# Linear attention and spectral mixing on one core: two tiles' sums placed ahead of the early rows, four filler products fewer, and the late rows gathered by two transfers

## The chip, the cores and the metric

The kernel runs on one core of one Trainium2 chip. A core has five engines with instruction streams of their own: TensorE (PE in the profile; its weight loads are PEld), VectorE (DVE), ScalarE (ACT), GpSimd (POOL) and SyncE (SP). Each engine takes its instructions in program order and waits on semaphores for the others. POOL and SP also issue DMA transfers, which 16 DMA engines of the core carry out. The metric is the device time of one execution in microseconds (us), the median over several; lower is better. TensorE's clock is granted by a throttle; the profile shows it as a share of full speed (PEclk).

## The reference

```python
def _attn_ref(q, k, v):                     # q, k, v: (8, 8, 576, 64)
    phi = lambda x: np.where(x > 0, x, np.exp(x) - 1.0) + 1.0
    q_p, k_p = phi(q), phi(k)
    kv = np.einsum('bhsd,bhse->bhde', k_p, v)
    num = np.einsum('bhsd,bhde->bhse', q_p, kv)
    den = np.einsum('bhsd,bhd->bhs', q_p, np.sum(k_p, axis=2))[..., None] + 1e-06
    return num / den

def _moe_ref(x, w_r, w_i, w_ch):            # x: (8, 576, 512), w_r, w_i: (64, 512, 512)
    X = np.fft.rfft(x, axis=1)
    Xr, Xi = np.real(X[:, :64]), np.imag(X[:, :64])
    Y = np.zeros_like(X)
    Y[:, :64] = (Xr @ w_r - Xi @ w_i) + 1j * (Xr @ w_i + Xi @ w_r)   # one 512x512 pair for each mode
    u = x + np.fft.irfft(Y, n=576, axis=1)
    return u + np.maximum(u @ w_ch, 0.0)    # (8, 576, 512), float32
```

The 64 modes' weights, w_r and w_i, are 64 x 2 x 1 MB of float32: 134 MB to be read once. The output is 9.4 MB.

## The kernel before

**Stages.** First the attention of the eight batches (lines 373 to 408), with the forward transform of its result into 64 modes. Then 32 pairs of modes: `mode_pair(p)` (L465) multiplies the spectrum by the weights of modes 2p and 2p+1. Weights come over POOL's DMA queue, which also turns them into bfloat16, into two rotating buffers. While weights are on their way, other work is done from a list, `work`, in slots after parts of each pair (`work_slot`, L427). That work rebuilds the attention output x, adds the inverse transform of the first 32 modes (`fold`), turns it (`turn_x`) and multiplies by w_ch (`channel_product`, kept as E). The last stage adds the modes 32 to 63 to x and to u @ w_ch, takes the rectifier and stores the output.

**Order.** Nearly all instructions are pinned to program order, so what stands earlier in the code is issued earlier on its engine. `keep_warm(n)` (L419) issues n products of 512 columns whose result nobody reads; in the profile they are the group at L422 (`zl<-wch,id`). `FILL[p]` says how many follow pair p, `WARM` how many follow each of the pieces in which the very last weights come.

**The last pair** (`last_pair`, L490) does modes 62 and 63. The weights of pair 31 come in eight transfers (`w_load_last`, L124): mode 62's two halves, mode 63's first half, and its second half in five pieces, `PIECES`, of two, two, two, one and one of the eight chunks. The steps on TensorE are: the early rows (`ahead_rows`, L920: the results of the modes 56 to 61, as rows in y and multiplied by w_ch in z, after VectorE has copied them into Y8 at L922); a slot of the list, whose first two items are the channel product and the first rows of the first pair of output tiles (`channels(0)` L807, `first_rows(0)` L900); the product of mode 62 (L435); a second slot with the same for the second pair of tiles; the picks (L458); three fillers; and then mode 63 piece by piece (L518, `y_last`), each piece after its weights have landed, with a filler after some.

**The late rows.** All late modes' rows must lie in one tile, YZ_all, ordered by batch, with y and z beside each other. Rows of modes 56 to 61 are gathered into it by two transfers (`ahead_gathers`, L940), one issued from SP and one from POOL, which wait for the third piece from the end. After mode 63 its rows are transposed (L978) and multiplied by w_ch (L984) into `last[0]` (y) and `last[1]` (z), and four transfers on POOL's queue (L994) bring the 32 rows of the modes 62 and 63 into YZ_all: z to both halves of the tile, then y to both. The output tiles of the first two batches do not read these rows from YZ_all but from `last` with their own selection matrix (`lead_sb`); the others read YZ_all (`add_inverse`, L762).

**The tail.** The tiles are finished in pairs: `channels` (L807), the late modes in z (L767), the rectifier on ACT (L1002, L817), the late modes in y (L767), the sum on VectorE (L1006, L841), and a store from SP's queue (L823, L829). The first four pairs are stored tile by tile in 256 KB, the others in 512 KB. There are 22 stores.

Of the kernel before, what the change touches and what calls it, by code (L numbers as in the profile page):

```python
# [11 lines left out]
F16 = mybir.dt.float16  # L12
# [31 lines left out]
def kernel(  # L44
# [10 lines left out]
    nc = tc.nc  # L55

    B, H, S, Dh = q.shape
    D = H * Dh
    NM = moe_w_r.shape[0]
    NHP = H // 2  # L60
    NDC = D // 128
# [8 lines left out]
    NA = NL - 2  # L70
    RA = 2 * B * NA
# [36 lines left out]
    pin = tc.keep_in_program_order  # L108
# [3 lines left out]
    LAST = NM // 2 - 1  # L112
# [41 lines left out]
    def rows_of(jj: int, base: int = 0):  # L154

        if jj < NJJ:
            return slice(base + jj, base + 512, NJJ)
        return slice(512, S) if base == 0 else slice(0, base)
# [252 lines left out]
    def w_get(p: int):  # L411
        if p not in w_in and p == LAST:
            w_load_last(wpool, "w", W_KEEP)
        elif p not in w_in:
            for half in range(2):
                w_load(p, half, wpool, "w", W_KEEP)
        return w_in[p]

    def keep_warm(n: int):  # L419

        for _ in range(n):
            pin(nc.tensor.matmul(last_ps[0], id16, wch16[:, 0, :]))  # L422
# [4 lines left out]
    def work_slot(p: int, name: str):  # L427
        for _ in range(slots.get((p, name), 0)):
            if work:
                work.pop(0)()  # L430

    def product(P, x, n: int, w, dc: int, n_dc: int):
        c = dc % NDC * 32
        pin(
            nc.tensor.matmul(  # L435
                P[c : c + n, :], x, w[:, dc, :],
                start=(dc < NDC), stop=(dc >= n_dc - NDC), tile_position=(0, c),
                skip_group_check=True,
            )
        )  # L440
# [24 lines left out]
    def mode_pair(p: int):  # L465
# [19 lines left out]
        work_slot(p, "end")  # L485
        keep_warm(FILL.get(p, 0))

    WARM = {2: 0, 4: 1, 6: 1, 7: 0, 8: 1}

    def last_pair():  # L490
        xl = ystage.tile([128, NDL, 2 * B], BF16, name="xl")
        for h in range(2):
            src = xt_v[:, (2 * h + 1) * NDC : (2 * h + 2) * NDC, :, :, LAST]
            pin(
                nc.vector.tensor_copy(
                    out=xl[:, h * NDC : h * NDC + NDC], in_=src.rearrange("p c t b -> p c (t b)")
                )
            )
        w = w_get(LAST)
        kk = NM - 2  # L500
        ahead_rows()
        work_slot(LAST, "start")
        P = psW.tile([128, D], F32, tag="P", bufs=2, name=f"P{kk}")
        for dc in range(NDL):
            n = 32 if dc < NDC else 2 * B
            product(P, xt_cols(dc, kk, n), n, w, dc, NDL)
        st = evacuate(kk, P)
        work_slot(LAST, "mid")
        picks(kk, st, 1)
        pin(nc.vector.tensor_copy(out=Y8[:, :, NA, :], in_=yt_ps[:, :, NA, :]))  # L510
        ahead_gathers()
        keep_warm(3)
        y_last = psW.tile([128, NDC, 2 * B], F32, tag="P", bufs=2, name="y_last")
        for piece in PIECES:
            for dc in range(piece.start, piece.stop):
                for ec in range(NDC):
                    pin(
                        nc.tensor.matmul(  # L518
                            y_last[:, ec, :], w[:, NDL + dc, ec * 128 : ec * 128 + 128], xl[:, dc, :],
                            start=(dc == 0 and ec == 0), stop=(dc == NDL - 1), skip_group_check=True,  # L520
                        )
                    )
            keep_warm(WARM[piece.stop])
        nc.vector.tensor_copy(out=Y8[:, :, NL - 1, :], in_=y_last)
# [12 lines left out]


    n_early = n_keep + n_pre
    FILL = {**{p: 7 for p in range(5, 16)}, **{p: 7 for p in range(18, 27)}, 27: 7, 28: 10, 29: 12, 30: 2}  # L540
    ystage = ctx.enter_context(tc.tile_pool(name="ystage", bufs=1, side="right"))
    inv_sb = ystage.tile([2 * NM, S], F16, name="inv_sb")
    inv2_sb = ystage.tile([128, S], F16, name="inv2_sb")
# [1 line left out]
    lead_sb = [ystage.tile([128, S], F16, name=f"lead{b}_sb") for b in range(N_LEAD)]  # L545
# [3 lines left out]
    Y8 = ystage.tile([128, NDC, NL, 2 * B], F16, name="Y8")  # L549
# [24 lines left out]
    yt_ps = None  # L574
# [9 lines left out]
    sW = ctx.enter_context(tc.tile_pool(name="sW", bufs=1))  # L584
# [11 lines left out]
    def x_of(t: int):  # L596
        if t < B * NJJ:
            return x_main[t // NJJ][:, t % NJJ, :]
        i = t - B * NJJ
        return x_tail[i // 2][:, i % 2, :]  # L600
# [13 lines left out]
    last_ps = []  # L614
# [65 lines left out]
        return ye_at[0]  # L680

    x16w, xTw = {}, {}

    def fold(t: int):

        x = x_of(t)
        acc = bank(f"ya{t}")
        for b, jj, orow in parts_of(t):
            pin(
                nc.tensor.matmul(  # L690
                    acc[orow, :], inv_sb[: 2 * NF, rows_of(jj, BASE[b % 2])], YE[b][: 2 * NF, :]
                )
            )
        pin(nc.vector.tensor_tensor(out=x, in0=acc, in1=x, op=ALU.add))  # L694
        x16w[t] = sW.tile([128, D], F16, tag="x16w", bufs=2, name=f"x16w{t}")
        pin(nc.scalar.copy(out=x16w[t], in_=x))  # L696

    def turn_x(t: int):
# [63 lines left out]
    def add_inverse(n: int, half: int, tiles_of=(0, 1)):  # L762

        def mm(i, orow, l, r):
            on_bank(
                n, {i},
                nc.tensor.matmul(  # L767
                    accs[n][orow, i], l, r, start=False, stop=True, skip_group_check=True
                ),
            )  # L770

        for i in tiles_of:
            for b, jj, orow in parts_of(pairs[n][i]):
                sel_rows = rows_of(jj, BASE[b % 2])
                if n < 2 * N_LEAD:
                    mm(i, orow, lead_sb[b][:, sel_rows], last[half])
                else:
                    g = HALVES[i]
                    mm(i, orow, inv2_sb[g, sel_rows], YZ[b][g, half, :])
# [139 lines left out]

    def ahead_rows():  # L920

        pin(nc.vector.tensor_copy(out=Y8[:, :, 0:NA, :], in_=yt_ps[:, :, 0:NA, :]))  # L922
        ya_ps = psW.tile([128, NDC, 128], F16, tag="P", bufs=2, name="ya_ps")
        za_ps = psW.tile([128, D], F32, tag="P", bufs=2, name="za_ps")
        for ec in range(NDC):
            pin(nc.tensor.transpose(ya_ps[:, ec, :], rows[ec], id16))
        for ec in range(NDC):
            pin(
                nc.tensor.matmul(
                    za_ps, rows[ec], wch16[:, ec, :], start=(ec == 0), stop=(ec == NDC - 1)  # L930
                )
            )
        pin(nc.scalar.copy(out=ahead[0:RA, 0, :], in_=ya_ps[0:RA].rearrange("p c r -> p (c r)")))
        pin(nc.scalar.copy(out=ahead[0:RA, 1, :], in_=za_ps[0:RA]))

    def late_at(h: int, r0: int, n: int):
        at = 64 * h + r0 // B * (NF // NL)
        return YZ_all[at : 64 * h + 64 : NF // NL][0 : n // B]
# [21 lines left out]
    for n in range(N_PRE):  # L960
# [1 line left out]
    last_pair()  # L962


    last = [
        sW.tile([128, D], F16, tag="x16w", bufs=2, name="last_y"),
        sW.tile([128, NDC, 128], F16, tag="xTw", bufs=2, name="last_z").rearrange("p c r -> p (c r)"),
    ]
    z1_ps = psW.tile([128, NDC, 8, 2 * B], F32, tag="yt", bufs=1, name="z1l")
    y_ps = [  # L970
        psW.tile([128, NDC, 128], F16, tag="P", bufs=2, name=f"ypl{h}")[:, 0 : NDC // 2] for h in range(2)
    ]
    y0 = psW.tile([128, D], F32, tag="P", bufs=2, name="y0l")
    last_ps.append(z1_ps.rearrange("p c m n -> p (c m n)"))
    hw = D // 2
    COLS = [slice(h * hw, h * hw + hw) for h in range(2)]
    for ec in range(NDC):
        pin(nc.tensor.transpose(y_ps[ec // 2][:, ec % 2, :], rows[ec], id16))  # L978
    pin(nc.scalar.copy(out=last[0][:, COLS[0]], in_=y_ps[0].rearrange("p c r -> p (c r)")))
    pin(nc.vector.tensor_copy(out=last[0][:, COLS[1]], in_=y_ps[1].rearrange("p c r -> p (c r)")))  # L980
    for h in range(2):
        for ec in range(NDC):
            pin(
                nc.tensor.matmul(  # L984
                    last_ps[h][:, 0:hw], rows[ec], wch16[:, ec, COLS[h]],
                    start=(ec == 0), stop=(ec == NDC - 1),
                )
            )
        pin(nc.scalar.copy(out=last[1][:, COLS[h]], in_=last_ps[h][:, 0:hw]))
    pin(nc.tensor.matmul(y0, lead_sb[0][:, rows_of(0)], last[0]))  # L990
    pin(nc.vector.tensor_tensor(out=x_of(0), in0=y0, in1=x_of(0), op=ALU.add))
    for z in (1, 0):
        for h in range(2):
            nc.gpsimd.dma_start(out=late_at(h, RA, 128 - RA)[:, :, z, :], in_=last[z][RA:128])  # L994
    psW.release()
    acc_pools.append(
        tc.alloc_tile_pool(name="psT1", bufs=1, space=PSUM, side="left", reuse_waits="tile")
# [11 lines left out]
    def sums_of(n: int, tiles_of):  # L1009
        channels(n, tiles_of)  # L1010
        add_inverse(n, 1, tiles_of)
        for i in tiles_of:
# [6 lines left out]
            out=x_of(0), in0=accs[0][:, 0], scalar=0.0, in1=x_of(0), op0=ALU.max, op1=ALU.add  # L1019
# [50 lines left out]
```

## Time and profile before

| what | value |
|---|---|
| median of three runs | 420.98 us (420.90 to 421.04) |
| profiled execution, its own time | 421.02 us |
| its span in the profile | 419.2 us |
| mean granted TensorE clock | 0.837 |
| PE busy | 313.1 us, 75% of the span, 3143 instructions |
| DVE busy | 231.2 us, 55% |
| ACT busy | 155.1 us, 37% |
| POOL's DMA queue | 81.54 MB, 93.6% of 16 engines' span |
| SP's DMA queue | 11.16 MB, 7.2% |
| read from and written to memory | 163.93 MB, 9.44 MB |

The profile is one execution. "Busy" sums an engine's instructions; matmuls are pipelined and their ends modelled, so a busy PE isn't a PE at its peak. The strip divides the span into 40 slices of 10.5 us and shows tenths. The chain of waits is followed back from the last instruction, at each step to what released it. The timeline lists instructions in order of time with start, length, engine, line, operation, tiles (out<-in) and how many were merged, and in brackets how long the engine stood idle before and what ended it.

### The profile page before, as it was taken

What the parts mean: (1) busy time and instruction counts of PE and PEld (TensorE: products, weight loads), DVE (VectorE), ACT (ScalarE), POOL (GpSimd) and SP (SyncE); (2) the same over time, 40 slices, a digit from 0 to 9 for tenths busy, and PEclk for the clock granted to TensorE, in tenths of its full rate; (3) what the DMA queues carried; (4) which work ended last, traced back from release to release, by engine and by line L of the source; (5) the groups of instructions that cost most, each with busy time, mean ns of one, the idle gap of its engine ahead of it and who ended that gap; (6) DMA issues with size and microseconds to landing.
All of it is one profiled execution on the core that took longest, in us unless ns stands there. A gap on an engine that the chain in (4) does not pass through costs nothing.

```text
span 419.2 us, 7479 instructions
## 1 busy us (share of the span) xinstructions
PE 313.1 (75%) x3143; PEld 162.6 (39%) x3143; DVE 231.2 (55%) x511; ACT 155.1 (37%) x255; POOL 59.1 (14%) x104
## 2 busy tenths in 40 slices
PE   0369997999607774777666686988788877998993
PEld 0257775877301331223222233333333323363421
DVE  4588899695414572464645353464446443532794
ACT  4687797854201020000000233344353423231783
POOL 4222224210011211111111111111111111130200
PEclk9999998579855687555856599899999989799998
DMA  8999999999999999999999999999999999999698
GB/s 217 212 212 217 209 224 203 228 208 222 213 227 205 223 219 208 224 217 209 220 216 214 220 209 220 217 212 220 220 208 220 217 213 220 213 202 177 229 394 331
DMA packets 17229, 93.17 MB, mean 222 GB/s; under 512 B 2284, under 2 KB 3196, under 8 KB 13036
## 3 DMA queue, kind: packets, MB, share of 16 engines
q0 software_dynamic: 12688, 81.54, 93.6%
q1 hardware_dynamic: 4508, 11.16, 7.2%
q8 instruction: 24, 0.39, 0.3%
q14 instruction: 9, 0.07, 0.0%
HBM read 163.93 MB, written 9.44 MB: 414 GB/s over the span
## 4 chain that ended last, share of the span: by engine, by line
DMA 60%; PE 24%; DVE 6%; issue 3%; ACT 3%; POOL 3%; DVEq 0%; ACTq 0%; POOLq 0%
DMA w<-in_moe_w_i_dram 48%; DMA pick_sb<-row_pick 8%; PE P L435 7%; DMA k<-in_k_dram 3%; PE acc L767 3%; PE kvp L260 2%; PE zl L422 2%; PE acc L807 2%; PE eps L713 2%; DVE x L296 1%; POOL w L119 1%; PE z L733 1%; ACT ke L211 1%; PE yb L752 1%; ACT qT L247 1%
## 5 line engine op out<-in xcount | busy, mean ns | idle before, releaser
L435 PE MATMUL P<-w,xz 128*32 128x512 bf16 x496 | 42.9, 479 | 39.2 <-DMA w<-in_moe_w_i_dram 37.0
L452 ACT CAST ys<-P 128x512 f16<-128x512 f32 x15 | 8.8, 586 | 133.7 <-PE P L435 133.7
L422 PE MATMUL zl<-wch,id 128*128 128x512 f16 x177 | 55.9, 466 | 0.0
L119 POOL DMA_DIRECT2D w<-in_moe_w_r_dram x31 | 17.1, 552 | 247.8 <-PE P L435 222.1
L450 DVE CAST ys<-P 128x512 f16<-128x512 f32 x17 | 11.8, 692 | 51.6 <-PE P L435 51.6
L713 PE MATMUL eps<-wch,xTw 128*128 128x512 f16 x144 | 39.7, 402 | 0.0
L435 PEld LDWEIGHTS <-xz 128*32 128x32 bf16 x496 | 12.5, 108 | 64.4 <-DMA w<-in_moe_w_i_dram 40.9
L166 PEld LDWEIGHTS <-qT 64*128 64x128 f16 (+1 forms) x640 | 22.6, 122 | 30.7 <-issue 16.0
L696 ACT CAST x16w<-x_main 128x512 f16<-128x512 f32 x32 | 19.8, 618 | 37.4 <-DVE x_main L694 37.4
L694 DVE TENSOR_TENSOR x_main<-ya,x_main 128x512 f32<-128x512 f32 x32 | 22.0, 689 | 18.4 <-PE ya L690 18.2
L260 PE MATMUL kvp<-vpad,ke 32*128 32x130 f16 x576 | 24.3, 261 | 8.9 <-ACT qT L247 6.0
L445 DVE COPY xz<-xt_c 64x256 bf16<-64x256 bf16 x62 | 23.0, 372 | 11.2 <-PE P L435 10.4
L721 ACT CAST E<-eps 128x512 f16<-128x512 f32 (+1 forms) x40 | 21.2, 540 | 19.0 <-PE eps L713 19.0
L422 PEld LDWEIGHTS <-id 128*128 128x128 f16 x177 | 18.2, 113 | 24.3 <-issue 13.8
L260 PEld LDWEIGHTS <-ke 32*128 32x128 f16 x576 | 22.1, 115 | 10.6 <-issue 8.1
L166 PE MATMUL nw<-kv_sb,qT 64*128 64x65 f16 (+1 forms) x320 | 17.9, 230 | 10.1 <-DVE x_tail L657 4.7
L296 DVE TENSOR_TENSOR x<-num,rd 128x512 f16<-128x512 f32 x32 | 22.1, 692 | 1.1
L240 PE MATMUL qTp<-id,qe 128*128 128x128 f16 x144 | 14.1, 276 | 11.5 <-DVE qe L224 9.5
L458 PE MATMUL yt<-pick_sb,ys 128*128 128x32 f16 (+1 forms) x128 | 8.6, 183 | 17.3 <-DMA pick_sb<-row_pick 9.7
L705 DVE COPY xTw<-xTp 128x512 f16<-128x512 f16 x36 | 15.0, 416 | 11.5 <-PE xTp L703 11.4
L657 DVE TENSOR_TENSOR x_main<-nw,rd 128x256 f32<-128x256 f32 x32 | 11.2, 416 | 17.6 <-PE nw L166 17.6
L211 ACT ACTIVATE qe<-q 128x1152 f16<-128x1152 f16 (+1 forms) x16 | 17.9, 1157 | 8.3 <-DMA q<-in_q_dram 8.2
(129 smaller groups left out, 509.1 us busy)
## 6 DMA issues: line engine op xcount, KB each, us to landing
w<-in_moe_w_r_dram POOLq DMA_DIRECT2D x31, 1024.0 KB, 13.1
w<-in_moe_w_i_dram POOLq DMA_DIRECT2D x31, 1024.0 KB, 17.5
out_dram<-x_main SPq DMA_DIRECT2D x12, 512.0 KB, 3.7
k<-in_k_dram POOLq DMA_DIRECT2D x8, 576.0 KB, 12.8
v<-in_v_dram POOLq DMA_DIRECT2D x8, 576.0 KB, 14.5
q<-in_q_dram POOLq DMA_DIRECT2D x7, 576.0 KB, 12.6
out_dram<-x_main SPq DMA_DIRECT2D x8, 256.0 KB, 3.0
q<-in_q_dram SPq DMA_DIRECT2D x2, 576.0 KB, 4.5
```

What stands on the lines that cost most here:

```text
L119: nc.gpsimd.dma_start(out=w_in[p][half::2], in_=two.rearrange("g (r dc) e -> (g r) dc e", dc=NDW))
L166: mm = nc.tensor.matmul(num[hpo][orow, c0 : c0 + 65], qT[rows, hpp, h2, cols], kv_sb[rows, hpp, h2, :])
L211: pin(nc.scalar.activation(out=ev[:, c], in_=heads(nm, b, c), func=AF.Exp))
L260: nc.tensor.matmul(kv_ps[:, h2, 0:130], phi["k", b][r0 : r0 + 32, j // NJ, j % NJ].rearrange("p o d -> p (o d)"), vp[r0 : r0 + 32, :, j, 0 ...
L296: nc.vector.tensor_tensor(out=dst.rearrange("p (o c d) -> p o c d", o=2, c=4), in0=nv[:, :, :, 0:64], in1=rden.unsqueeze(3).broadcast_to([ ...
L422: pin(nc.tensor.matmul(last_ps[0], id16, wch16[:, 0, :]))
L435: nc.tensor.matmul(P[c : c + n, :], x, w[:, dc, :], start=(dc < NDC), stop=(dc >= n_dc - NDC), tile_position=(0, c), skip_group_check=True,)
L445: pin(nc.vector.tensor_copy(out=xz[p % 2][HALVES[h], :, h, :], in_=src))
L694: pin(nc.vector.tensor_tensor(out=x, in0=acc, in1=x, op=ALU.add))
L696: pin(nc.scalar.copy(out=x16w[t], in_=x))
L713: nc.tensor.matmul(e_ps, xT[:, c, :], wch16[:, c, :], start=(c == 0), stop=(c == NDC - 1))
L721: pin(nc.scalar.copy(out=dst, in_=e_ps[:, cols]))
```

## The change

Five edits. `ahead_rows` gives up its first instruction, VectorE's copy into Y8, which `last_pair` now issues itself, followed by the first slot of the list and only then by `ahead_rows`: on TensorE two channel products and two first-row products stand ahead of the early rows' transposes and products. Four fillers go: the two after pair 30 (`FILL[30]`), one of the three ahead of mode 63, and the one after its third piece (`WARM[6]`). The two rotating buffers that `fold` fills become two halves of one tile, `x16_pair`. The last rows' y and z become two halves of one tile, `last`, that follows in its place. Its 32 late rows go into YZ_all by two transfers, each with y and z together in runs of 2 KB, one from SP's queue (ahead of the stores) and one from POOL's, instead of four on POOL's in runs of 1 KB.

```diff
-    WARM = {2: 0, 4: 1, 6: 1, 7: 0, 8: 1}
+    WARM = {2: 0, 4: 1, 6: 0, 7: 0, 8: 1}
...
         w = w_get(LAST)
         kk = NM - 2
+        pin(nc.vector.tensor_copy(out=Y8[:, :, 0:NA, :], in_=yt_ps[:, :, 0:NA, :]))
+        work_slot(LAST, "start")
         ahead_rows()
-        work_slot(LAST, "start")
...
         ahead_gathers()
-        keep_warm(3)
+        keep_warm(2)
...
-    FILL = {**{p: 7 for p in range(5, 16)}, **{p: 7 for p in range(18, 27)}, 27: 7, 28: 10, 29: 12, 30: 2}
+    FILL = {**{p: 7 for p in range(5, 16)}, **{p: 7 for p in range(18, 27)}, 27: 7, 28: 10, 29: 12, 30: 0}
...
+    x16_pair = sW.tile([128, 2, D], F16, tag="x16w", bufs=1, name="x16_pair")
+    x16_at: list = []
...
-        x16w[t] = sW.tile([128, D], F16, tag="x16w", bufs=2, name=f"x16w{t}")
+        x16w[t] = x16_pair[:, len(x16_at) % 2, :]
+        x16_at.append(t)
...
     def ahead_rows():
-        pin(nc.vector.tensor_copy(out=Y8[:, :, 0:NA, :], in_=yt_ps[:, :, 0:NA, :]))
...
-    last = [
-        sW.tile([128, D], F16, tag="x16w", bufs=2, name="last_y"),
-        sW.tile([128, NDC, 128], F16, tag="xTw", bufs=2, name="last_z").rearrange("p c r -> p (c r)"),
-    ]
+    last = sW.tile([128, 2, D], F16, tag="x16w", bufs=1, name="last")
...
-    for z in (1, 0):
-        for h in range(2):
-            nc.gpsimd.dma_start(out=late_at(h, RA, 128 - RA)[:, :, z, :], in_=last[z][RA:128])
+    for h, eng in enumerate((nc.sync, nc.gpsimd)):
+        eng.dma_start(
+            out=late_at(h, RA, 128 - RA).rearrange("r b z d -> r b (z d)"),
+            in_=last[RA:128].rearrange("p z d -> p (z d)"),
+        )
```

Uses of `last[0]` and `last[1]` become `last[:, 0, ...]` and `last[:, 1, ...]`. TensorE's instructions go from 6288 to 6280, four products and their four weight loads; the other engines compute with as many as before, POOL issues three transfers fewer and SP one more.

## The prediction

> **What bounds the kernel now.** I read the forty-slice strip of the page first, then the chain of waits around the last weights, then the timeline there.
>
> ```profile
> span 419.2 us, 7479 instructions
> PEclk9999998579855687555856599899999989799998
> DMA  8999999999999999999999999999999999999698
> ```
>
> DMA is full from the first slice to the 37th, dips in one slice (10.5 us each; 388 to 398 us), and is full again. So weight loads set the time to about 388 us, the output stores set it from about 399 us, and only the bridge between them hangs on TensorE. The change touches that bridge. Chain of waits (start, length, what):
>
> ```profile
> 374.21 12.73 DMA w<-in_moe_w_i_dram
> ...
> 388.83 0.40 PE ypl L978 x4
> 389.22 0.44 PE zl L984 x4
> 389.66 0.45 PE z1l L984 x4
> ...
> 390.56 0.59 PE acc L767 x2
> ```
>
> The DMA that ends the first row brings the weights of the second of five pieces (landed 386.94). Between y_last (done 388.52) and the first product of the tail (390.56) lie 1.1 us of matmuls whose length follows the clock (four transposes, eight 256-column products, 388.83 to 389.93), one DVE cast (0.24 us), one ACT copy (0.38 us) and drains. The timeline shows what precedes them:
>
> ```profile
> 386.99 0.36 PE L518 MATMUL y_last<-xl,w 128*128 128x16 bf16 x8 [0.18 <-DMA w<-in_moe_w_i_dram]
> 387.20 0.38 PE L422 MATMUL zl<-wch,id 128*128 128x512 f16 x1
> 388.01 0.49 PE L518 MATMUL y_last<-xl,w 128*128 128x16 bf16 x8
> ```
>
> Eight of these take 0.36 us in one go; the last eight take 0.49, so there is a hole of 0.13 us before the final piece. In 250 ns stretches DMA still moves 12 GB/s in 387.75 to 388.00 and nothing after. The weights end this wait, not the filler at 387.80.
>
> **Fillers and moved sums, if the clock holds.** The change drops four fillers of 0.216 us (twelve in a row start 0.216 us apart): two at 381.02, one of three at 385.80, the one at 387.80. It moves the first pair's two channel products and two first-row products (382.92 to 383.88, about 1.0 us) into 381.02 to about 382.0, where TensorE had two fillers and then 0.2 us idle for Y8 (copied 381.21 to 381.77). Their inputs date from before 367 us, so they add no wait. Behind them ya and za start some 0.2 us later; ACT's copies of those feed the early gathers, which go at 387.80 and 388.30, after a weight piece: over 3 us of cover. The half-width product of the last pair comes 0.7 us earlier, the first weight-piece product could start near 385.5 (0.7 plus one filler earlier) instead of 386.46, but pieces keep arriving as before: the second began 386.99 behind DMA. The cover is the landing of the weights; without it the gain would be 0.95 us plus the filler at 387.80, 0.2. So between 0 and 1.15 us; I take 0, since the second piece and the last are both shown waiting.
>
> **Tile layout.** x16_pair has the bytes of the two old buffers, the casts at L696 keep their count (32 of 0.618 us) and waits, and lie where weights set the pace: 0. The last rows in one tile: same copies, 0.
>
> **Late gathers.** Before: four POOL issues (1.20 + 1.17 us, 390.80 to 393.16), 32 KB each. After: one on SP, one on POOL, 64 KB each.
>
> ```profile
> out_dram<-x_main SPq DMA_DIRECT2D x2, 512.0 KB, 2.7
> out_dram<-x_main SPq DMA_DIRECT2D x4, 512.0 KB, 3.9
> YZ_all<-last_z POOLq DMA_DIRECT2D x2, 32.0 KB, 2.9
> YZ_all<-last_y POOLq DMA_DIRECT2D x2, 32.0 KB, 3.3
> YZ_all<-rows_ahead POOLq DMA_DIRECT2D x1, 192.0 KB, 5.1
> ```
>
> (The DMA view; first row for stores issued in 398 to 400, second for 409 to 414.5; last figure is us to landing.) SP now waits for ACT's last copy (390.51) ahead of all 22 stores. Its 96-row gather took 0.97 us to issue; even at that, 32 rows are out by 391.5, before the first store's 391.91. TensorE's first read of late rows (394.93) now needs y as well as z. POOL's transfer goes at 390.80; between 3.3 us (32 KB) and 5.1 (192 KB), by size 3.7, it lands at 394.5: 0.4 us to spare; at 5.1 TensorE would lose 1.0. Gain: y's 64 KB leave the store stage, 0.16 us at its 400 GB/s, both 0.33. But stores issued at 398 still land in 2.7 us, unqueued; the 3.9 at the end is a queue built later, by pairs coming each 1.21 us (399.49 to 413.99, twelve steps) against the 1.31 that 512 KB take at 400 GB/s. So early DMA time is not yet the limit and I take 0 (ends -0.3 and +1.0).
>
> Sum so far: 0, 421.0.
>
> **The clock.** Fillers hold the granted clock. It changes only on a grid of 3.41 us in this trace. Four stretches of that grid (us, PE busy, PEld, DVE, ACT, POOL, PEclk, DMA, GB/s):
>
> ```profile
> 316.75:320.16 3.41, 1.54 (x11) 0.51 (x12) 1.22 (x3) 1.31 (x3) 0.00 (x0) 1.00 1.06 226
> 320.16:323.57 3.41, 3.41 (x34) 1.51 (x27) 2.04 (x4) 0.83 (x2) 1.07 (x2) 1.00 1.06 226
> 350.88:354.29 3.41, 1.86 (x16) 1.06 (x13) 1.42 (x4) 0.79 (x2) 1.07 (x2) 1.00 1.06 226
> 354.29:357.71 3.42, 2.90 (x8) 0.99 (x8) 2.63 (x5) 0.38 (x1) 0.00 (x0) 0.50 1.04 220
> ```
>
> Busy 1.54 us kept the clock, busy 1.86 lost it. What decides is columns streamed, weighted by the share of the array: a full 512-column product counts 0.216 us, four 32-wide ones side by side 0.216 together, a 128-column transpose 0.054, a 32-column pick 0.013. First stretch: fillers from 316.39 on, seven in a row, leave 1.15 us in it, and one group of four at 319.94 adds 0.22: 1.37 of 3.41, 0.40: kept. Third: four products at 352.73 (0.86), four transposes (0.22), four picks (0.05): 1.13, 0.33: halved. Summed so over all stretches, ten drops follow shares up to 0.34, the 58 that kept full clock have 0.38 or more, and a halved clock came back after 0.75 or more.
>
> The Trainium skill says in "TensorE: Matmul & The Clock Gate", section "Why this matters for your kernels", that an idle gap over about 3 us drops the clock. By that the change is safe (its longest gap is near 1 us) and the time 421.0. The trace speaks against it: the lost stretch above has no gap over 0.85 us, another (337.23 to 340.64) none over 2.18.
>
> Now the bridge. Before, the stretch 385.01 to 388.43 holds five fillers and a bit (1.15), two half-array products (0.22), 32 small products of 16 columns (0.0067 each, 0.22) and picks: 1.6 of 3.41, 0.47. After: three fillers and a bit (0.72), the small ones, picks: 0.96, 0.28. The moved products lie before it. Sliding the grid: before never falls below 0.47; after it is at 0.35 or less for ends between 387.5 and 389.4, lowest 0.22: 2 of 3.41 us, and marginal at 386.9 to 387.2. So 0.6 to 0.7 of all runs lose the clock, if the phase is free (the trace shows one phase; three times within 0.14 us say that the old kernel didn't care).
>
> The unknown is a 16-column product: 0.0067 by columns or its 0.025 step? By step the lowest sum is 0.39, kept. Columns explain all 119 stretches, but so does a floor of 25 ns; a fixed 10 ns added to every matmul does not. I take columns.
>
> Price: with the end at 388.43, the 1.1 us of transposes and products take 2.2, TensorE reaches the tail at 391.7 instead of 390.56, 0.1 more until 391.84, 0.1 for longer drains: 1.3 us. The stretch itself then holds about 0.8, so full clock returns. Other phases: 0.85 to 1.6. All of it passes to the end, since stores follow TensorE from 391.91 and their queue only builds after 399. 421.0 + 1.3 = 422.3 (profiled 421.02, median 420.98: no difference).
>
> **Rivals.**
> Clock holds: small products count by step, or most runs have a kind phase. For it: the 0.39 bound; against: columns fit without a floor. All parts then cost 0: 420.9, from 420.6 to 421.2.
> Two half stretches: the first holds under 0.75 (0.77 for an end at 387.0, so close), the second runs the tail at half clock; it adds 3.41 / 2, less overlap: 2.3 to 2.9 in all, 423.5.
> Gathers late: POOL's lands at 395.9, TensorE loses 1.0: 422.0. Against: the ahead transfer with 5.1 was six times the size.
> Other side: the last weights are not what ends the wait in ordinary runs. Then the earlier product chain counts, up to 1.1 us, from the point where weights land 0.9 us before 388.2: 419.9. Against: the hole of 0.13 us and DMA activity to 388.
>
> **How the numbers follow.** Columns count: 0.78; a median over few runs then falls among the halved ones in 0.72 of cases: 0.56, of which one stretch 0.45 (own range 421.8 to 422.7), two 0.11. Gathers late 0.04. Clock holds 0.29. Earlier chain 0.11. A measurement of this kernel can tell about 0.2% (0.84 us) from no change: slower 0.60, same 0.29, faster 0.11. Range 420.6 to 423.5: it leaves out the earlier chain and the upper part of two stretches.
>
> **What would show it.** Granted clock 0.5 in some stretch between 387 and 393; y_last's last eight still at 388.0 to 388.5; z products 0.2 us apart rather than 0.11; first L767 near 391.8; last store issued 1.3 us later. Wrong: clock 1.00 throughout and first L767 at 390.5 (clock holds), or y_last done before 388 (weights not the limit), or TensorE waiting for a gather at 394.9.

## The result, and the profile after

| | before | after |
|---|---|---|
| median of 22 runs each, same chip | 420.95 us (420.44 to 422.21) | 422.12 us (420.85 to 422.56) |
| ratio after to before, 95% interval | | 1.002 [1.0013, 1.0028] |
| profiled execution, its own time | 421.02 us | 420.90 us |
| its span | 419.2 us | 419.1 us |

The median rose by 1.2 us, 0.2 us below the forecast. (The ratio in the table lies near that of the means; the two medians alone give 1.0028.) It is not a kernel that is 1.2 us slower each time: its executions fall into two groups with nothing between, 8 of 22 at 420.85 to 421.35 and 14 at 421.95 to 422.56 (medians 421.0 and 422.23). Of the kernel before one of 22 lies above 421.6. The profiled execution of the changed kernel is one of the lower group, so it shows the bridge with the clock held. Its strip (span, granted clock, DMA, in slices of 10.5 us):

```profile
span 419.1 us, 7469 instructions
PEclk9999999579855658665655599899899998899997
DMA  8999999999999999999999999999999999998698
```

DMA dips in the same slices as before, between the weights and the stores. Its chain of waits through the bridge (start, length, what):

```profile
373.06 13.76 DMA w<-in_moe_w_i_dram
...
388.15 0.05 issue
388.20 0.27 PE y_last L519 x4
...
389.18 0.44 PE zl L984 x4
389.61 0.45 PE z1l L984 x4
...
390.51 1.02 PE acc L771 x4
```

Four fillers are gone and two sums moved, and the tail begins at 390.51 instead of 390.56. The timeline of the same execution says where the freed time went (in brackets the idle time ahead of the instruction and what ended it):

```profile
383.16 0.66 PE L435 MATMUL P<-w,xt_c 128*32 128x512 bf16 x8 [0.57 <-DMA w<-in_moe_w_i_dram]
386.35 0.34 PE L519 MATMUL y_last<-xl,w 128*128 128x16 bf16 x8 [0.81 <-DMA w<-in_moe_w_i_dram]
386.87 0.36 PE L519 MATMUL y_last<-xl,w 128*128 128x16 bf16 x8 [0.17 <-DMA w<-in_moe_w_i_dram]
```

TensorE reaches the bridge earlier and waits 0.57, 0.81 and 0.17 us for weights that land about when they landed before (the second piece at 386.82 instead of 386.94). Nothing is gained, and TensorE is emptier. Whether that matters depends on where the grid of the clock lies. In this execution the stretches were (us, PE busy, PEld, DVE, ACT, POOL, PEclk, DMA, GB/s)

```profile
382.80:386.22 3.42, 2.39 (x18) 0.65 (x18) 0.92 (x2) 0.41 (x1) 0.00 (x0) 1.00 0.78 148
386.22:389.63 3.41, 2.90 (x44) 1.99 (x45) 0.52 (x2) 0.37 (x1) 0.63 (x1) 1.00 0.29 53
389.63:393.04 3.41, 3.14 (x16) 1.54 (x15) 2.45 (x4) 2.86 (x6) 0.63 (x1) 1.00 0.55 168
```

with 0.41 and 0.43 of the array-columns in the first two, counted as in the prediction: kept.

### The profile page after: what moved, and what is told of

Read it like the earlier page. It is cut to its first block, busy times and chain, and to the rows that moved or that the text cites. A ratio compares the mean times of both kernels' runs of the same rounds, so it can differ in the third digit from the quotient of the medians.

```text
span 419.1 us, 7469 instructions
## 1 busy us (share of the span) xinstructions
PE 315.5 (75%) x3139; PEld 163.7 (39%) x3139; DVE 231.4 (55%) x511; ACT 155.3 (37%) x255; POOL 57.3 (14%) x101
## 4 chain that ended last, share of the span: by engine, by line
DMA 66%; PE 22%; DVE 3%; issue 2%; POOL 2%; ACT 2%; DVEq 0%; POOLq 0%; ACTq 0%
DMA w<-in_moe_w_i_dram 53%; DMA pick_sb<-row_pick 8%; PE P L435 6%; DMA k<-in_k_dram 5%; PE acc L771 3%; PE kvp L260 2%; PE acc L811 2%; POOL w L119 1%; PE z L737 1%; ACT ke L211 1%; PE xf L358 1%; PE qTp L240 1%; PE zl L422 1%; PE num L166 1%; PE yb L756 1%
## 5 line engine op out<-in xcount | busy, mean ns | idle before, releaser
L700 ACT CAST x_pair<-x_main 128x512 f16<-128x512 f32 x32 | 19.8, 618 | 37.7 <-DVE x_main L697 37.7
L240 PE MATMUL qTp<-id,qe 128*128 128x128 f16 x144 | 15.1, 289 | 10.7 <-DVE qe L224 9.7
```

## The experiments

In all tables and texts "upper" is an execution above 421.6 us. Every kernel was run beside the kernel before, on the same chip. Of the kernel before 6 of 97 runs were upper: 1 of 22 beside the changed kernel, 4 of 29 beside e1 to e4, 1 of 33 beside e5 to e8 and none of 13 beside e9 to e11. The changed kernel itself was run in the first of these four groups alone; e4 comes nearest to it in the second.

| run | edit | median (range), us | ratio to before, 95% | upper |
|---|---|---|---|---|
| changed kernel | | 422.12 (420.85 to 422.56) | 1.0020 [1.0013, 1.0028] | 14 of 22 |
| e1 | four fillers back | 421.23 (420.79 to 422.53) | 1.0010 [1.0001, 1.0020] | 3 of 12 |
| e2 | before, four fillers out | 420.84 (420.72 to 422.08) | 0.9997 [0.9987, 1.0006] | 1 of 11 |
| e3 | before, six fillers cut small | 423.42 (422.30 to 424.37) | 1.0055 [1.0038, 1.0072] | 6 of 6 |
| e4 | old late gathers | 421.95 (420.75 to 422.38) | 1.0012 [1.0001, 1.0023] | 7 of 12 |
| e5 | move undone | 421.08 (420.71 to 422.31) | 1.0006 [0.9997, 1.0015] | 1 of 11 |
| e6 | move undone, four fillers early | 421.00 (420.70 to 422.31) | 1.0005 [0.9996, 1.0013] | 1 of 11 |
| e7 | six fillers in the gap | 420.95 (420.75 to 422.32) | 1.0008 [0.9999, 1.0016] | 2 of 11 |
| e8 | e7 and 48 small products far ahead | 421.82 (421.57 to 422.04) | 1.0023 [1.0014, 1.0032] | 10 of 11, one group |
| e9 | three fillers behind the moved sums | 422.10 (420.54 to 422.80) | 1.0023 [1.0009, 1.0036] | 4 of 6 |
| e10 | no fillers in the bridge | 422.38 (421.12 to 423.47) | 1.0035 [1.0023, 1.0048] | 6 of 7 |
| e11 | e10, move undone | 422.31 (422.19 to 423.65) | 1.0041 [1.0029, 1.0053] | 5 of 5 |

**e4, the late gathers alone undone.**

```diff
-    for h, eng in enumerate((nc.sync, nc.gpsimd)):
-        eng.dma_start(
-            out=late_at(h, RA, 128 - RA).rearrange("r b z d -> r b (z d)"),
-            in_=last[RA:128].rearrange("p z d -> p (z d)"),
-        )
+    for z in (1, 0):
+        for h in range(2):
+            nc.gpsimd.dma_start(out=late_at(h, RA, 128 - RA)[:, :, z, :], in_=last[RA:128, z, :])
```

> The changed kernel with the four gathers of before on POOL (z to both halves, then y), all else as changed. Share theory: the gathers are worth nothing, so the same two groups as the changed kernel, 0.55 to 0.75 of the executions at 422.2 and the rest at 420.95, median 422.1. If the SP gather or the collision of two 64 KB transfers on few DMA engines cost the time, all executions are near 420.95.

The same two groups in about the same shares: the gathers don't make the upper group. They aren't free, though. A run's time less its span is 1.79 us in e4 (median of its runs) and 1.77 or 1.78 in the kernel before beside e1 to e11, but 2.07 in the changed kernel and 2.07 to 2.15 in e1 and e5 to e11, which all have the new gathers. These 0.3 us lie outside the span. The eight profiles with 2.0 us or more there show a transfer of 8 KB of program code behind the span's end, at 420.6 to 422.4 us; the five with 1.8 or less show none. Why the new gathers bring it on isn't shown.

This kernel's profile (422.01 us) fell into the upper group, so it shows what the changed kernel's own profile didn't. Its stretches, on the grid as it lay in this execution:

```profile
386.06:389.47 3.41, 2.74 (x43) 1.87 (x44) 0.51 (x2) 0.37 (x1) 0.63 (x1) 1.00 0.27 48
389.47:392.89 3.42, 3.39 (x12) 1.35 (x10) 1.39 (x3) 1.80 (x4) 1.77 (x3) 0.50 0.39 118
392.89:396.30 3.41, 3.41 (x17) 1.51 (x15) 3.17 (x5) 2.92 (x6) 0.60 (x2) 1.00 0.76 262
```

and its chain of waits:

```profile
388.17 0.27 PE y_last L519 x4
...
389.15 0.44 PE zl L984 x4
389.58 0.83 PE z1l L984 x4
390.42 0.43 PE y0l L990
...
390.88 2.22 PE acc L771 x5
```

Up to 389.15 it is the changed kernel's profile to within 0.03 us. The first stretch holds a share of 0.39 by columns, and at its end the clock goes to 0.50 for one stretch. The second set of four z products takes 0.83 instead of 0.45, and the five products that open the tail take 2.22 and end at 393.10; with the clock held they end at 391.94. The 1.16 us are still there at the last store, issued at 415.10 instead of 413.94, and at the end of the span (420.2 against 419.1).

**e3, the kernel before with products too small to count.** The six fillers of mode 63 (three behind the picks, three between the pieces) become eight products of 16 columns each: TensorE as busy by instructions, but with few columns.

```diff
+    def keep_warm_small(n: int):
+        for _ in range(8 * n):
+            pin(nc.tensor.matmul(last_ps[0][:, 0:16], id16, wch16[:, 0, 0:16]))
...
-        keep_warm(3)
+        keep_warm_small(3)
...
-            keep_warm(WARM[piece.stop])
+            keep_warm_small(WARM[piece.stop])
```

> The kernel before with each of its six fillers around mode 63 replaced by eight 16-column products of the same weights: about the same busy time (8 x 0.025 against 0.216 us), no longer idle gap, but 0.053 us of columns in place of 0.216. By columns: lowest sum 0.19, under 0.335 for 0.59 of the phases, so 0.6 of the executions near 422.2 and the median there. By the step of a product, or by busy time, or by idle gaps: lowest sum 0.59, no execution loses the clock, median 420.95.

All six runs are upper, without any move and with the old gathers. Stretches of its profile (423.43 us):

```profile
385.36:388.78 3.42, 2.46 (x72) 2.02 (x69) 0.23 (x1) 0.00 (x0) 0.63 (x1) 1.00 0.37 65
388.78:392.19 3.41, 3.38 (x16) 1.85 (x15) 0.98 (x2) 1.34 (x4) 0.61 (x1) 0.50 0.40 115
```

TensorE runs 72 products, is busy 2.46 of 3.42 us and loses the clock, where 1.54 us with few but wide products had kept it in the prediction's first stretch. By the 0.025 us step between small products the share would be 0.49, well above the 0.38 from which the clock was kept; by columns it is 0.15. Columns count. But the time is 2.5 us above before, twice what one lost stretch costs; e8 takes that up.

**e10, no fillers in the bridge.** The changed kernel without the two behind the picks and the two between the pieces.

```diff
-    WARM = {2: 0, 4: 1, 6: 0, 7: 0, 8: 1}
+    WARM = {2: 0, 4: 0, 6: 0, 7: 0, 8: 0}
...
-        keep_warm(2)
```

> The changed kernel without any filler around the last mode's products (the two behind the picks and the two between the pieces are out). By columns the stretches that end at 385.6 to 389.9 are all below 0.37, lowest 0.06: wider than the grid of 3.41 us, so that each phase has at least one border there. Theory of the clock by share: all or nearly all runs (10 or 11 of 11) in the upper group, 421.9 to 423.2, some with two stretches lost; none or one at 420.9. Rival, the fillers cost TensorE's time and keep nothing: 420.6 to 421.0, faster than the changed kernel. The idle-gap reading (the clock falls only behind more than 3 us without work): idle pieces stay below 2 us, so 420.9 in one group.

Six of seven are upper. Its timeline and its stretches:

```profile
386.34 0.35 PE L518 MATMUL y_last<-xl,w 128*128 128x16 bf16 x8 [1.10 <-DMA w<-in_moe_w_i_dram]
386.87 0.36 PE L518 MATMUL y_last<-xl,w 128*128 128x16 bf16 x8 [0.18 <-DMA w<-in_moe_w_i_dram]
387.48 0.91 PE L518 MATMUL y_last<-xl,w 128*128 128x16 bf16 x16 [0.25 <-DMA w<-in_moe_w_i_dram]
```

```profile
384.90:388.31 3.41, 1.80 (x37) 1.31 (x36) 0.22 (x1) 0.00 (x0) 0.12 (x1) 1.00 0.49 85
388.31:391.73 3.42, 3.07 (x18) 1.88 (x15) 0.76 (x3) 1.12 (x3) 0.51 (x2) 0.50 0.38 115
```

y_last ends at 388.39, against 388.47 with the fillers: the weights end it, and the fillers cost at most 0.08 us. And a stretch whose longest pause is 1.10 us, with a share of 0.07 by columns, loses the clock.

**e1 and e2, the fillers alone.** e1 puts the four fillers back into the changed kernel, e2 takes them out of the kernel before, with the sums where they were. The diff is e1's; e2's is its reverse, in the kernel before.

```diff
-    WARM = {2: 0, 4: 1, 6: 0, 7: 0, 8: 1}
+    WARM = {2: 0, 4: 1, 6: 1, 7: 0, 8: 1}
...
-        keep_warm(2)
+        keep_warm(3)
...
-    FILL = {**{p: 7 for p in range(5, 16)}, **{p: 7 for p in range(18, 27)}, 27: 7, 28: 10, 29: 12, 30: 0}
+    FILL = {**{p: 7 for p in range(5, 16)}, **{p: 7 for p in range(18, 27)}, 27: 7, 28: 10, 29: 12, 30: 2}
```

> The changed kernel with its four fillers put back; the moved sums, the tile layout and the two gathers stay. Share theory (an execution loses the clock when a 3.41 us stretch that ends between 387 and 389.5 has under about 0.35 of the array's columns streaming): lowest sliding sum 0.31, under 0.375 for a quarter of all phases, under 0.335 for a tenth; so 0.10 to 0.26 of the executions near 422.2, the rest and the median at 420.9 to 421.0. If the moved sums or the gathers made the executions at 422.2, they stay at 0.6 of all and the median stays near 422.1.

> The kernel before with the same four fillers taken out and nothing else. Share theory: the two first-row products of the second pair still lie late (385.1 to 385.6), the lowest sum is 0.34, under 0.375 for 0.23 of all phases, never under 0.335; so between none and a quarter of the executions at 422.2, median 420.95. If the number of fillers alone decided (order of no account), 0.6 of the executions are at 422.2. If the gathers did it, none.

e1's share of upper runs came out as expected; its median is 0.2 to 0.3 us above the expected one, as much as lies outside the span with the new gathers. e2's count came out too, but not for the reason given, a lowest share of 0.34: in its profile (420.72 us) the share slides as low through the bridge as in the changed kernel (0.22 at 388.75 against 0.20), and yet 1 of 11 is upper. So taking the fillers out is not enough. e4 rules out the gathers; the moved sums, which the prediction had priced at nothing, belong to the cause. A hint came from e1's profile, where the clock was lost earlier and was back in time:

```profile
376.97:380.38 3.41, 1.37 (x21) 0.55 (x22) 1.04 (x4) 0.00 (x0) 0.53 (x1) 1.00 0.97 202
380.38:383.79 3.41, 3.41 (x12) 1.15 (x11) 0.54 (x1) 0.37 (x1) 0.00 (x0) 0.50 1.05 210
383.79:387.21 3.42, 3.42 (x36) 1.27 (x34) 0.92 (x2) 0.79 (x2) 0.00 (x0) 1.00 0.63 113
```

A border in the bad part of the bridge means one 6.83 us earlier, near 381, where the sums lay or didn't lie. That made a theory (A: a hole at 381 loses the clock where the weights cover it, and the late TensorE then fills the bridge), which e5 and e6 test.

**e5 and e6, the move undone, and its place filled.**

```diff
-        work_slot(LAST, "start")
         ahead_rows()
+        work_slot(LAST, "start")
```

That is e5, in the changed kernel (Y8's copy goes back into `ahead_rows` too). e6 is the same with four fillers where the moved sums stood:

```diff
-    FILL = {**{p: 7 for p in range(5, 16)}, **{p: 7 for p in range(18, 27)}, 27: 7, 28: 10, 29: 12, 30: 0}
+    FILL = {**{p: 7 for p in range(5, 16)}, **{p: 7 for p in range(18, 27)}, 27: 7, 28: 10, 29: 12, 30: 4}
```

> The changed kernel with one part undone: the copy of Y8 and the four sums of the first two preloaded pairs go back to where the kernel before has them, two sums behind the early rows (about 382.1 us) and two behind the last pair's products; the four fillers stay out and the late rows go by two transfers of 2 KB runs. In the profile of the kernel before with only the fillers out (the same order on TensorE) the stretches of 3.41 us that end at 381.0 to 381.25 hold a share of array-columns of 0.37, where the changed kernel has 0.45 to 0.49; the stretches that end at 387.5 to 389.4 hold at most 0.37 in both (lowest 0.20 and 0.22). Theory A, hole by hole: a grid that puts a border into 387.5 to 389.4 has the border two stretches before in 380.7 to 382.6, so in part of the runs the clock is lost there, where the wait for the weights covers it, and is back before the bridge; then fewer than in the changed kernel end in the upper group (121 over the lower 420.9): 1 to 4 of about 12, median 420.9. Theory B, the fillers alone decide: 0.55 to 0.65 in the upper group, 6 to 8 of 12, median 421.9 to 422.2, as in the changed kernel. Theory C, the moved sums cost by something else than the clock (order, banks of the accumulators): no upper group at all and 420.9.

> The same, with four fillers of 512 columns behind mode pair 30, at about 380.3 us, where the changed kernel has its four moved sums; the two fillers around the last mode's products stay out. TensorE has 0.65 us of idle time there in the profile, so two tenths of a microsecond are pushed on, ahead of weights that land 0.6 to 0.8 us after TensorE asks for them. Theory A: the early hole is filled again (stretches that end at 380.3 to 383.7 rise from 0.37 to about 0.6), no clock is lost there, and the bridge is as empty as before: 0.5 to 0.65 of the runs in the upper group near 422.1, median 421.5 to 422.2, although four fillers are added to the kernel of the run beside it. Theory B, the fillers around the bridge alone decide: 0.55 to 0.65 here and in the run beside it alike. Theory C, it is the move by something else than the clock: as the run beside it, 420.9. That the added fillers themselves keep the clock: fewer in the upper group than beside it.

e5 repeats e2: with the fillers out and the sums not moved, 1 of 11 is upper. e6 speaks against theory A, which asked for half the runs in the upper group. It is a weak test, though: its fillers pushed the work behind them into the bridge (picks at 385.31 instead of 384.62), where the share then is at 0.37 or less only for ends from 388.0 to 388.5. e5's timeline shows what the move removes:

```profile
379.84 0.27 PE L458 MATMUL yt<-pick_sb,ys 128*128 128x32 f16 x4 [0.80 <-DVE ys L450]
380.76 0.40 PE L929 MATMUL ya_ps<-id,Y 128*128 128x128 f16 x4 [0.65 <-DVE Y L925]
```

TensorE stands 0.65 us ahead of the early rows, until VectorE has copied Y8. The moved sums lie in that pause, and all that follows comes earlier. This is theory D: where TensorE is behind the weights, the pause leaves 0.65 us of array work more for the bridge.

**e7, more fillers in the gap.** In the changed kernel:

```diff
-        keep_warm(2)
+        keep_warm(6)
```

> The changed kernel with six fillers in place of two behind the last mode's picks (at about 385 us), where TensorE waits 0.8 us for weights; nothing else is changed. By columns the lowest stretch of the bridge rises from 0.20 to about 0.43. Theory of the clock by share of array-columns, lost at about 0.37 and kept at 0.41: no run in the upper group, all at 420.7 to 421.4, median 420.9; the two groups of the changed kernel are gone. Rival, that the four moved sums or the transfers have a price of their own: median 421.3 or more with the upper group still there. Rival, that four more products delay the last mode: first inverse product after 390.7 and 421.1 to 421.5 in one group.

Two of 11 are upper, not none, but the median is back at 420.95, with the move, the tile layout and the new gathers all in place. So the upper group of the changed kernel is the emptied bridge, not a price of these parts.

**e9, fillers behind the moved sums,** and **e11, e10 with the move undone** (e10's edit and e5's together). The diff is e9's, in the changed kernel:

```diff
         work_slot(LAST, "start")
+        keep_warm(3)
         ahead_rows()
```

> The changed kernel with three fillers of 512 columns (0.65 us at full clock) behind the moved sums and ahead of the early rows, at about 381.3 us; nothing else is changed. In the kernel with the move undone TensorE stands 0.65 us before the early rows, until VectorE has copied Y8; the moved sums lie in this pause, so that the changed kernel comes to the bridge up to 0.65 us of work lighter. Theory D, the work left for the bridge: both changes together empty it, in the executions in which TensorE is behind the weights too; the three fillers put the 0.65 us back, the stretches that end at 387.5 to 389.4 rise, and the upper group shrinks to the 1 or 2 of 11 that the kernel with the move undone and the kernel before show; median 420.9 to 421.2. Theory A, hole by hole: the stretches around 380 to 383 are fuller still, no clock is lost there, and the bridge, at 385 and later, is as empty as in the changed kernel where the weights are awaited: 0.5 to 0.65 in the upper group, median 421.5 to 422.2. Rival, that the moved sums cost by another way than the clock: as the changed kernel, 422.1, too.

> The run beside it with the move of the two pairs' sums undone: no fillers around the last mode's products, the sums where the kernel before has them. By columns the stretches that end at 385.6 to 389.5 are below 0.37 here as well. Theory D, the work left for the bridge: without fillers the 0.65 us of the pause no longer fill it, so that most runs are in the upper group, 7 to 11 of 11, median 421.9 to 422.6, where the kernel with two fillers kept and the move undone has 1 of 11. Theory E, the moved sums alone decide and the fillers don't matter without them: 0 to 2 of 11 in the upper group, median 420.9.

e9 is inconclusive: 4 of 6 upper, theory A's number, but its profile (422.01 us) got there by a third way:

```profile
376.31:379.72 3.41, 1.52 (x19) 0.33 (x16) 0.38 (x1) 0.00 (x0) 0.53 (x1) 1.00 1.01 211
379.72:383.14 3.42, 3.05 (x11) 0.82 (x12) 1.20 (x4) 0.00 (x0) 0.00 (x0) 0.50 1.01 204
383.14:386.55 3.41, 3.41 (x18) 1.07 (x15) 0.00 (x0) 1.16 (x2) 0.00 (x0) 0.50 0.75 140
```

The clock goes at 379.72 (share 0.34, behind a wait of 1.45 us for pair 30's weights), is not back at 383.14 (0.71), and returns at 386.55 (0.89). TensorE, with more to do at half speed, is now what the bridge waits for: y_last ends at 389.46 and the tail begins 1 us late, with the clock whole. e11, with 5 of 5 upper, refutes that the moved sums alone decide (theory E). Its profile and e10's are both of executions in which TensorE comes late to pair 30 (379.21 and 379.07, no wait), and they make a pair. e11's first piece, to be read against e10's above:

```profile
386.56 0.34 PE L517 MATMUL y_last<-xl,w 128*128 128x16 bf16 x8 [0.48 <-DMA w<-in_moe_w_i_dram]
```

It waits 0.48 us for its weights, e10's 1.10. Adding the four fillers' columns to both profiles gives, for ends at 387.5 to 388.25, shares of 0.41 to 0.49 in e11's order and 0.27 to 0.36 in e10's. For ends at 388.5 to 389.0 e11's order is down to about 0.35 as well, where both outcomes were seen. That is what theory D needs in the main, but it is an estimate from two profiles.

What it leaves open: e2's and e5's profiles are of early executions in which the bridge is as empty as in the changed kernel, and how many of the timed runs were early isn't known. The 13 profiles say something on it. Of the seven whose grid has a border between 387.9 and 389.1, six are late: TensorE reaches pair 30 at 378.6 us or later and doesn't wait (e3's is the exception). The six with a border between 386.0 and 387.3 are all early: 378.0 to 378.3 us, after a wait of 0.1 to 1.5 us. The phase of the grid and TensorE's lateness go together, so an early profile tells little of what a border at 388 to 389 would meet. That fits the 1 of 11 of e2 and e5, but no run tests it.

**e8, code.** e3's profile has one transfer of program code more than the others, among the stores. So 48 small products were put behind mode pairs 5 to 15 and 18 of e7, at 143 to 271 us, almost 150 us and more ahead of the end.

```diff
+    def small(n: int):
+        for _ in range(n):
+            pin(nc.tensor.matmul(last_ps[0][:, 0:16], id16, wch16[:, 0, 0:16]))
...
         keep_warm(FILL.get(p, 0))
+        small(4 if p in (*range(5, 16), 18) else 0)
```

> The run beside it (six fillers in the gap, clock kept) with 48 products of 16 columns added far ahead of the end: four behind each of the mode pairs 5 to 15 and 18, where TensorE waits for weights (some 0.1 to 0.2 us behind each). It has nothing to do with the clock of the bridge; it makes TensorE's program 96 instructions longer. In the kernel whose fillers were cut into small products (84 instructions more) the profile shows one 16 KB transfer of code more than in the others, at 409.5 us among the stores, 1.5 us long on one of the sixteen DMA engines, and 1.2 us more at the end than its clock explains. Theory, that this transfer is what the end pays for: one such transfer again between 400 and 412 us, and 421.8 to 422.4 in one group, 1.0 to 1.4 above the run beside it. Rival, that the clock cost more there than in the changed kernel (the whole bridge at half speed): as the run beside it, 420.8 to 421.0.

One group again, 0.87 us above e7. The DMA view of 400 to 412 us (queue, kind: packets, MB, share of 16 engines) of e3, and then of e8:

```profile
q8 instruction: 1, 0.02, 0.8%
```

```profile
q8 instruction: 1, 0.02, 0.5%
```

The changed kernel and e7 have no such line there. One packet of 16 KB is carried by one of the 16 engines: 0.8% of 16 x 12 us is 1.5 us, 0.5% is 1.0 us. SP's timeline of e8, then of e7:

```profile
413.67 0.51 SPq L833 DMA_DIRECT2D out_dram<-x_main  x1
```

```profile
414.01 0.43 SPq L827 DMA_DIRECT2D out_dram<-x_main  x1
```

e8 issues its last store 0.34 us earlier, and its span ends 0.4 us later (419.7 against 419.3). The stores are queued at 400 GB/s by then. Those of 400 to 420 us in the DMA view, of e8 and then of e7 (the last figure is the median time to landing):

```profile
out_dram<-x_main SPq DMA_DIRECT2D x10, 512.0 KB, 4.8
```

```profile
out_dram<-x_main SPq DMA_DIRECT2D x10, 512.0 KB, 3.7
```

One by one, the store issued at 404 us lands after 3.6 us in both. Code is fetched at 406.9 in e8, and every store issued from 407.6 on lands after 4.8 or 4.9 us, where e7's take 3.7 to 4.2. In e3 code is fetched at 409.5; the store issued at 406.6 takes 3.7 us, those from 409.0 on 4.9 to 5.5. The step is about as long as the fetch (0.93 us in e8, 1.51 in e3) and it stays to the end. That each store waits for its piece on the one engine that fetched code is argued; the trace doesn't tell these engines apart.

## Why the prediction was right, and where it was not

**Fillers and moved sums, clock aside: nothing.** Right. With the clock held the changed kernel lies at 421.0; the last four products of y_last start at 388.20 in the changed kernel and at 388.17 in e4. This is the sum with the clock left out; what the moved sums do through the clock stands below. The rival that lets the earlier chain count is out: with all of the bridge's fillers gone TensorE still ends on the weights (e10).

**Tile layout, late gathers: nothing.** Right inside the span: e4 shows the old transfers to leave the two groups as they are, and no wait for a gather appeared at 394.9. But the new gathers go with 0.3 us outside the span, for which the sum had no term (its ends for the gathers, -0.3 and +1.0, hold it). e5 and e7, with the new layout and transfers, have medians of 421.08 and 420.95, 0.27 and 0.14 us above the kernel before beside them (420.81).

**The clock, by columns streamed.** Right, and the unknown was taken from the right side: e3's 16-column products kept TensorE busy and did not keep the clock. The later profiles widen its border a little: drops followed shares up to 0.39, and the lowest share that kept the clock is 0.34. The rule of the Trainium skill that the prediction weighed, an idle gap of some 3 us ("TensorE: Matmul & The Clock Gate", section "Why this matters for your kernels"), does not describe e10, whose longest pause in the lost stretch was 1.10 us. The same page's Part 1 on the clock gate says that the window of 3413 ns runs freely and doesn't start with the kernel; that the runs do show, as the borders nearest to 388 us lie anywhere from 386.55 to 389.65 in the profiles.

**Price 1.3 us.** Nearly right: the groups' medians are 1.23 us apart, e4's tail is 1.16 us late, and all of it reaches the end, as said. e10 and e11, whose borders (388.31 and 388.58) lie near the 388.43 that the prediction took, begin the tail at 391.49 and 391.70, where it had 391.7 to 391.84.

**How often: 0.6 to 0.7.** Right in number (14 of 22), but part of the agreement is luck. That "before never falls below 0.47" was read from one execution and taken for all: 6 of 97 runs of that kernel are upper. The share of the changed kernel came from sliding the grid over one timeline, as if the timeline didn't depend on the phase; the profiles show the two to go together. And e2 and e5, whose profiles slide as low, have 1 of 11 each.

The moved sums, "between 0 and 1.15 us; I take 0", had an effect through the clock. The prediction saw a part of it: of the 0.64 us of columns by which its two sums for the bridge differ, 0.22 are half-array products that come earlier. It didn't see that the moved sums fill a pause of 0.65 us and so bring TensorE to the bridge with less left to do. That the missing fillers alone aren't enough is shown by e2 and e5 (2 of 22 upper, against 21 of 34 in the changed kernel and e4). That the move alone isn't enough rests on e1, 3 of 12 against e4's 7 of 12 beside it, which is thin. That the pause is the reason is argued.

**Two half stretches.** The changed kernel has no run above 422.56, so this rival did not appear; e10's and e11's slowest (423.47 and 423.65) lie where it was priced, but no profile shows what they lost.

## What to carry to other kernels

A wait that is off the critical path can still be where the clock for the next stage is decided: before fillers are taken out or work is moved into a pause, slide the clock's window over what is left and count columns, not busy time. A grid that runs freely turns a marginal window into two groups of times, so one profile, and one median over three runs, can show either. And where the end is bound by queued stores, look at when the program's code is fetched: a longer program moves that.

## What the runs showed of the hardware

In these runs a block of code cost time when its fetch fell among queued stores: 96 instructions more, placed far from the end, added 0.87 us (e8), and 84 more, in e3, brought a fetch of 1.5 us there, about the 1.3 us that the clock leaves unexplained. The Trainium skill says in "Runtime: NRT & Kernel Launch", section "Instruction fetch mechanics", that code is fetched in 16 KiB blocks by a queue of its own and that crossing a boundary is mostly hidden. The size agrees with the packet here. Every kernel's profile has such a block between 387 and 395 us, around the dip between weights and stores; e3's and e8's alone have another among the queued stores, and there it was not hidden.

The clock can also be lost well ahead of the bridge, behind a wait of 1.4 us for pair 30's weights (e1, e9), and whether that costs nothing or a microsecond depends on whether the next stretch reaches about 0.75: 0.81 in e1, back at once and a span of 419.1 us; 0.71 in e9, a second stretch at half speed.

The clock's records begin late, at 50.5 us in the profile of before and at 55.1 in that of the changed kernel, and until then the strip's 9s only stand for missing records. In the profile of before a product of 128 columns takes 0.31 us ahead of 50.5 us, as in later stretches at half clock, and 0.22 at full clock. So the mean granted clock of 0.837 is too high.
